# Block 3's y read back in two sets of partitions, the ranking's products behind the first second product, and the logits copied in two tiles

## The chip, the cores and the metric

The kernel runs on one core of one Trainium2 chip. The metric is the device time of one execution in microseconds (us); three runs were timed, and their median is the time before. TensorE (PE) does the matrix products, VectorE (DVE) and ScalarE (ACT) the elementwise work, GpSimd (POOL) the indirect transfers, and SyncE (SP) issues nearly all other DMAs. Each engine works through its own instructions in order.

## The reference, cut to what matters

```
h   = x + conv(layernorm(x)) + D_skip * layernorm(x)      # x: 2048 tokens x 512, S4D kernel applied by FFT
xt  = layernorm(h)
g   = softmax(xt @ wg)                                    # 8 experts
e   = argmax(g)                                           # one expert for each token
out = h + (gate / gate) * gelu(xt @ w1[e]) @ w2[e]        # w1: 512 x 1792, w2: 1792 x 512 for each expert
```

## The kernel before, in words

Two layers follow each other in one program. The convolution works on four blocks of 128 channels. For a block, four steps `c_s1` (matmul line L502) and eight steps `c_s2` (L521) transform the S4D kernel, `c_z` (DVE, L712) multiplies with the transformed input that `c_load` (SP, L705) read into a tile `u`, `c_ia` (PE, L719 and L720) transforms back, `c_ys` copies the result out of PSUM (ACT or DVE, L725), and `c_yst` (SP, L728) stores it in the DRAM scratch `yd`. The eight pieces of a block are called rc 0 to 7, and the store of rc fills 16 consecutive rows of the layout in which y is read back. In block 3 the pieces are made in the order 5, 7, 2, 6, 3, 0, 1, 4.

When all eight stores of the block have landed, `c_y1` (SP, L751) reads y back in four quarters q of 512 KB, each a tile of 128 partitions. `c_ib` (PE, L756, four matmuls) does the last transform of a quarter, `c_add` (DVE, L759) adds it to the residual, and the routing work follows: `r_s4` and `r_ag` (DVE, L972 and L1018) gather statistics, `r_tr` (PE, L977) transposes, `r_ev` (ACT, L981) copies, `r_lg` (PE, L989) makes logits, and `r_hd` (SP, L1003) stores h in the scratch `hd`. Block 3's quarters go in the order 0, 2, 1, 3. Quarters of block 2 stand beside them.

Behind the last logits `r_le` (L995) copies them out of PSUM in two halves, one on ACT and one on DVE, into two halves of one tile; `r_lt` (PE, L1000) transposes them, `r_sd` (ACT, L1022) takes square roots of the variances, `r_rs` (DVE, L1025) inverts them, and `r_vs` (SP, L1077) stores mean and inverse deviation in `hd`. A chain on DVE and PE (L1053 to L1161) picks each token's expert and makes the row list `r_gi` of the first expert. `m_ga` (POOL, L1266) gathers the rows of that expert from `hd`, so it waits for the list and for all stores into `hd`.

Then come eight experts. `m_w1` and `m_w2` (SP, L1349 and L1359) load weights, `m_h` (ACT, L1363) and `m_l` (DVE, L1367) split them in two parts, `m_ln`, `m_tr`, `m_xh` and `m_xl` (L1311, L1317, L1324, L1329) prepare the tokens, `m_g1` (PE, L1376 to L1378) makes first products, `m_ge`, `m_gh` and `m_gl` (L1381, L1384, L1388) the gelu and its split, and `m_g2` (PE, L1409 to L1411) second products. Beside the first expert the rest of the ranking is done: `r_B` and `r_M` (DVE, L1148 and L1169), `r_tb` (PE, L1176, 16 matmuls in two calls) and `r_ix` (DVE, L1180 to L1184), which gives the row lists of the other experts.

The order of the work is written out by hand. `ORD` gives every call of a step a number; all calls are emitted by rising number, and so each engine and each queue gets its order. `ON` chooses ACT (A) or DVE (V) for a copy. `FILL` puts filler matmuls (`idle`, PE, L930) ahead of a step: the number is a count of 128-column matmuls on zeros or the identity. The lists that `plan.add` takes as `r` and `w` name what a step reads and writes; the waits themselves follow from tiles and DRAM regions. A tile with a `tag` shares its `bufs` buffers with all tiles of that tag: the weights' tiles `h2` and `l2` give room to y of block 3, and `l2` to the logits.

Of the kernel before, what the change touches and what calls it, by code (L numbers as in the profile page):

```python
# [85 lines left out]
def _dram(ap, dims, off=0):  # L86
# [3 lines left out]
ORD = {  # L90
    'm_hold2': [932.5],
# [59 lines left out]
    'c_load': [422, 414, 333, 383, 331, 379, 398, 328, 530, 557, 455, 495, 452, 518, 439, 510, 591, 674, 686, 648, 657, 588, 645, 602,  # L151
# [4 lines left out]
    'c_s2': [437, 429, 373, 401, 370, 397, 413, 365, 555, 577, 486, 516, 489, 536, 481, 532, 635, 688, 710, 661, 678, 630, 656, 628, 805,  # L156
        809, 783, 795, 815, 774, 790, 779],
    'c_z': [444, 438, 386, 407, 375, 403, 428, 368, 563, 584, 496, 521, 491, 569, 485, 542, 641, 694, 714, 667, 691, 634, 664, 631, 810,
        812, 789, 799, 820, 777, 794, 785],
    'c_ia': [451, 446, 391, 417, 378, 408, 433, 374, 571, 593, 509, 526, 506, 579, 490, 552, 644, 703, 721, 680, 700, 639, 670, 652, 819,  # L160
        822, 798, 800, 825, 786, 811, 793],
    'c_ys': [456, 453, 399, 424, 384, 425, 441, 380, 582, 604, 517, 531, 512, 606, 499, 558, 654, 716, 730, 687, 709, 646, 675, 662, 823,
        826, 807, 813, 829, 788, 817, 796],
    'c_yst': [460, 458, 402, 426, 387, 430, 445, 381, 585, 607, 519, 533, 515, 610, 504, 561, 659, 717, 734, 690, 712, 651, 677, 663,
        824, 827, 808, 816, 830, 792, 818, 797],
# [17 lines left out]
    'r_ag': [863, 870.7, 870.6, 870.8],  # L183
# [3 lines left out]
    'm_w1': [818.5, 871, 871.5, 944, 951, 974, 979, 1009, 1032, 1050, 1088, 1099, 1120, 1146, 1166, 1186, 1202, 1222, 1247, 1269, 1291, 1313, 1331, 1347, 1367, 1393, 1416, 1436, 1452, 1474, 1490, 1522, 1539, 1559, 1580, 1596, 1617, 1633, 1662, 1678, 1698, 1723, 1736, 1757, 1773, 1801, 1817, 1840, 1852, 1873, 1889, 1905, 1932, 1948, 1968, 1978],  # L187
# [40 lines left out]
    'r_tb': [962.5, 974.5],  # L228
# [85 lines left out]
def s4d(tc, plan, env, cst, x, log_ar, a_im, c_re, c_im, log_dt, d_skip):  # L314
# [376 lines left out]
    cv = {}  # L691
# [69 lines left out]
    def conv(blk):  # L761
# [124 lines left out]
def moe(tc, plan, env, cst, wg, w1, w2, out):  # L886
# [578 lines left out]
    def tasks():  # L1465
# [4 lines left out]
        for b4 in range(4):  # L1470
# [3 lines left out]
            at("A", 0.2, r_sd, b4, w=[f"val/0/{b4}"], tab="sqrt")  # L1474
# [181 lines left out]
```

## Time and profile before

| what | us |
|---|---|
| median of the three timed runs | 726.71 |
| lowest and highest of them | 723.38 and 727.33 |
| the profiled execution's own time | 719.45 |
| span from its first to its last instruction | 717.4 |
| busy: PE, PE weight loads, DVE, ACT, POOL | 656.3, 575.3, 562.7, 455.7, 81.5 |

All rows below come from that one profiled execution. Times in them are microseconds from the start of the span. A PE row's length reaches over the start of the next row because matmuls are pipelined, so the spacing of starts tells what a group costs. "SPq" and "DMA_DIRECT2D" rows are the issuing of a transfer, not the transfer. A wait for several events is put down to the one that came last, as far as the trace can tell. A granted clock of 1.00 is TensorE's upper level (2.4 GHz), 0.50 the lower one (1.2 GHz).

### The profile page before, as it was taken

How to read it: one execution, taken by the hardware profiler on the slowest of the kernel's cores; microseconds unless marked ns; L12 is line 12 of the kernel's file. 1: busy time of each engine (PE TensorE's matmuls, PEld its weight loads, DVE VectorE, ACT ScalarE, POOL GpSimd, SP SyncE). 2: the span in 40 equal slices, each digit the busy share in tenths (PEclk: the TensorE clock that was granted, in tenths of full speed). 3: DMA queues.
4: the chain of work that ended last, by engine and by line, in shares of the span. 5: the costliest groups of instructions: out<-in, count | busy, mean ns of one | idle time of the engine just before them, and what ended most of it. 6: DMA issues, size and time to landing. Idle time of an engine off the chain costs nothing.

```text
span 717.4 us, 19936 instructions
## 1 busy us (share of the span) xinstructions
PE 656.3 (91%) x8192; PEld 575.3 (80%) x8192; DVE 562.7 (78%) x1055; ACT 455.7 (64%) x909; POOL 81.5 (11%) x65
## 2 busy tenths in 40 slices
PE   3588999988989999798889999999999999999995
PEld 2346898768778877596479999999999989898884
DVE  6999998889999999666689866766766687666752
ACT  6899999968974977312445555464555456566651
POOL 0000000000000000000006041050320402133201
PEclk9699999999999999999999999999999999999998
DMA  9994134566666678898767565465564667576620
GB/s 188 171 228 78 63 119 179 190 256 200 183 170 199 224 226 256 245 290 258 193 231 226 165 209 177 150 213 174 174 210 150 205 209 258 179 238 200 204 89 27
DMA packets 139255, 136.38 MB, mean 190 GB/s; under 512 B 42171, under 2 KB 108351, under 8 KB 138906
## 3 DMA queue, kind: packets, MB, share of 16 engines
q1 hardware_dynamic: 135674, 126.48, 60.7%
q0 software_dynamic: 3488, 8.60, 3.6%
q8 instruction: 65, 1.06, 0.6%
q14 instruction: 28, 0.23, 0.1%
HBM read 109.83 MB, written 29.52 MB: 194 GB/s over the span
## 4 chain that ended last, share of the span: by engine, by line
PE 43%; issue 17%; DVE 15%; DMA 12%; ACT 5%; SPq 4%; POOL 2%; POOLq 1%; DVEq 0%; ACTq 0%
DMA y<-yd_scratch 5%; PE ps_s L1376 4%; PE ps_s L1378 4%; PE ps_s L1377 4%; PE ps_kk L521 3%; DMA yd_scratch<-ys 3%; PE pk L652 2%; PE ps_ga L719 2%; DMA hr<-hd_scratch 2%; PE ps_ga L720 2%; PE ps_pl L930 2%; PE ps_kk L1409 2%; PE ps_s L502 2%; SPq L366 2%; PE ps_kk L1411 2%
## 5 line engine op out<-in xcount | busy, mean ns | idle before, releaser
L1367 DVE TENSOR_TENSOR l<-r,h 128x1024 fp32r<-128x1024 f32 x112 | 135.8, 1220 | 45.1 <-ACT h L1363 44.7
L1363 ACT CAST h<-r 128x1024 fp32r<-128x1024 f32 x112 | 116.1, 1047 | 45.7 <-PE ps_ga L1411 22.6
L1376 PE MATMUL ps_s<-xh,h 128*128 128x288 f32 (+5 forms) x448 | 128.7, 287 | 0.0
L1378 PE MATMUL ps_s<-xl,h 128*128 128x288 f32 (+5 forms) x448 | 127.3, 284 | 0.0
L1377 PE MATMUL ps_s<-xh,l 128*128 128x288 f32 (+5 forms) x448 | 127.1, 284 | 0.0
L1381 ACT ACTIVATE g<-ps_s 128x288 f32<-128x288 f32 (+5 forms) x112 | 43.6, 389 | 93.4 <-PE ps_s L1378 77.1
L1376 PEld LDWEIGHTS ps_s<-xh,h 128*128 128x128 f32 x448 | 84.5, 189 | 2.8 <-ACT xh L1324 0.2
L1377 PEld LDWEIGHTS ps_s<-xh,l 128*128 128x128 f32 x448 | 84.5, 189 | 2.2 <-issue 0.2
L1378 PEld LDWEIGHTS ps_s<-xl,h 128*128 128x128 f32 x448 | 84.4, 188 | 0.0
L1388 DVE TENSOR_TENSOR gl<-g,gh 128x288 fp32r<-128x288 f32 (+5 forms) x112 | 46.6, 426 | 23.0 <-ACT gh L1384 21.5
L719 PE MATMUL ps_ga<-u,mi 128*128 128x128 f32 x256 | 51.0, 281 | 3.1 <-issue 2.4
L1259 POOL DMA_INDIRECT out_dram<-ot,si x20 | 29.1, 1455 | 213.9 <-DVE ot L1426 210.4
L589 ACT ACTIVATE e<-alp 128x128 f32<-128x128 f32 x256 | 53.3, 313 | 0.0
L930 PE MATMUL ps_pl<-ident 128*128 128x512 f32 (+1 forms) x156 | 52.6, 483 | 0.0
L720 PE MATMUL ps_ga<-u,mi 128*128 128x128 f32 x256 | 49.8, 275 | 0.5 <-issue 0.5
L719 PEld LDWEIGHTS ps_ga<-u,mi 128*128 128x128 f32 x256 | 38.8, 191 | 7.7 <-issue 4.6
L930 PEld LDWEIGHTS ps_pl<-ident 128*128 128x128 f32 x156 | 27.5, 211 | 20.5 <-issue 19.7
L712 DVE TENSOR_TENSOR u<-ps_kk,u 128x1024 f32<-128x1024 f32 x32 | 38.5, 1216 | 4.9 <-PE ps_kk L521 4.8
L720 PEld LDWEIGHTS ps_ga<-u,mi 128*128 128x128 f32 x256 | 38.9, 192 | 0.6 <-issue 0.6
L1384 ACT CAST gh<-g 128x240 fp32r<-128x240 f32 (+5 forms) x82 | 33.6, 410 | 8.2 <-PE ps_ga L1410 5.4
L652 PE MATMUL pk<-e,vr 128*32 128x64 f32 x1024 | 36.1, 230 | 2.8 <-issue 1.6
L652 PE MATMUL pk<-wi,vi 128*32 128x64 f32 x1024 | 36.3, 228 | 2.2 <-DVE vi L628 1.1
(289 smaller groups left out, 1587.4 us busy)
## 6 DMA issues: line engine op xcount, KB each, us to landing
r<-in_B_w_dram SPq DMA_DIRECT2D x112, 512.0 KB, 3.8
u<-ud_scratch SPq DMA_DIRECT2D x32, 512.0 KB, 5.5
ud_scratch<-xn SPq DMA_DIRECT2D x16, 512.0 KB, 3.9
yd_scratch<-ys SPq DMA_DIRECT2D x32, 256.0 KB, 5.5
y<-yd_scratch SPq DMA_DIRECT2D x16, 512.0 KB, 5.0
xu<-in_A_u_dram SPq DMA_DIRECT2D x16, 256.0 KB, 7.2
xd_scratch<-in_A_u_dram SPq DMA_DIRECT2D x8, 512.0 KB, 7.2
xr<-xd_scratch SPq DMA_DIRECT2D x6, 512.0 KB, 4.1
```

The source lines that it names most:

```text
L589: A.activation(tb[blk, "e"][:, l // 2, :, l % 2], par(alp, blk), AF.Exp, scale=float(l))
L652: T.matmul(pk[32 * g:32 * g + 32, 64 * j:64 * j + 64], v[:, :, 8 * g + j], w[:, :, 8 * g + j, :], start=n == 0, stop=n == 1, skip_group_ch ...
L719: T.matmul(pa[:, c], mi[:, 4 * rc + rr, 64:192], z[:, 0, c], start=True, stop=False)
L720: T.matmul(pa[:, c], mi[:, 4 * rc + rr, 0:128], z[:, 1, c], start=False, stop=True)
L930: T.matmul(p[:, 0:128 * k], w, _view(ident, [[0, k], [1, 128]]), start=first, stop=True, skip_group_check=True)
L1363: A.copy(tile_(("h" + n, e, f), list(r.shape), F32R, pool="wp", name="h" + n, bufs=3 if n == "1" else 2), r)
L1367: V.tensor_tensor(tile_(("l" + n, e, f), list(r.shape), F32R, pool="wp", name="l" + n, bufs=3 if n == "1" else 2), r, t_["h" + n, e, f].bi ...
L1376: T.matmul(o[:, 0:CAPS[e]], a, xh, start=c == 0, stop=False)
L1377: T.matmul(o[:, 0:CAPS[e]], b, xh, start=False, stop=False)
L1378: T.matmul(o[:, 0:CAPS[e]], a, xl, start=False, stop=c == 3)
L1381: A.activation(tile_(("g", e, f), [128, CAP], name="g", bufs=2)[:, 0:CAPS[e]], t_["pf", e, f][:, 0:CAPS[e]], AF.Gelu_apprx_tanh)
L1388: V.tensor_tensor(tile_(("gl", e, f), [128, CAP], F32R, name="gl", bufs=3)[:, 0:n], t_["g", e, f][:, 0:n], t_["gh", e, f][:, 0:n].bitcast( ...
```

## The change

1. In block 3 the pieces rc 2 and rc 4 change places: the order becomes 5, 7, 4, 6, 3, 0, 1, 2, so that the last three pieces fill rows 0 to 47 of y. Their loads and u tiles change places too. The copy `c_ys` of rc 4, now third, goes to DVE; that of rc 2, now last, was on DVE already.
2. Each quarter of block 3's y is read in two transfers. `c_ya` reads partitions 48 to 127 (320 KB), which rc 3 to 7 fill; for q 0, 2 and 1 ACT issues it (ahead of `m_h(0)`), for q 3 SP does, behind the last store. `c_y1` then reads partitions 0 to 47 (192 KB) on SP, where the whole reads stood.
3. `r_tr`, `r_ev` and `r_lg` of block 2's quarter 1 move from behind block 2's last additions to 766.5, 766.6 and 773.5, around the last `c_s1` of block 3. Two fillers of 3 (ahead of `c_s1` 15 and of block 3's first `c_s2`) go.
4. `r_sd` is one activation on all 16 columns behind `r_le` instead of four, the first of which stood among the quarters of block 3; a new `r_sq` on one column stands at 830.6, behind `m_h(0)`.
5. `r_le` writes two tiles, and both copies are on ACT.
6. `m_w1(2)`, the load of expert 0's third piece of w1, moves on SP's queue from ahead of `r_vs` to behind it (871.5 to 905.3).
7. `r_tb` moves from ahead of the first `m_g2` to behind it (962.5 to 969.5), its second call from ahead of the fifth `m_g1` to behind it (974.5 to 975.5).
8. In block 3, `r_lg` of q 0 goes behind the last `c_ib` (865 to 868.2), `r_s4` of q 1 behind the last `c_add` (866.5 to 869.5), the first `r_ag` from 863 to 864.5.

```
 ORD = {
+    'r_sq': [830.6],
+    'r_sd': [883.5],
+    'c_ya': [829.1, 829.3, 829.2, 830.3],
...
-    'r_sd': [863.4, 883.4, 883.3, 883.5],
...
 FILL = {
...
-    ('c_s1', 10): 5, ('c_s1', 11): 5, ('c_s2', 23): 4, ('c_ib', 9): 9, ('c_s1', 15): 3, ('c_s2', 29): 3, ('c_ib', 12): 4, ('r_p1', 0): 8,
+    ('c_s1', 10): 5, ('c_s1', 11): 5, ('c_s2', 23): 4, ('c_ib', 9): 9, ('c_ib', 12): 4, ('r_p1', 0): 8,
...
     def c_load(blk, rc):
-        u = cv["u1", blk, rc] = utile(blk == 3 and rc > 2)
+        u = cv["u1", blk, rc] = utile(blk == 3 and rc not in (0, 1, 4))
...
     def c_y1(blk, q):
 
         if blk < 3 and (blk, q) != (2, 3):
-            t = cv["y1", blk, q] = mp.tile([128, 2, 512], F32, name="y1")
-        else:
-            t = cv["y1", blk, q] = env["wp"].tile([128, 2, 512], F32, name="y3", tag=("h2", "l2")[q // 2], bufs=2)
-        nc.sync.dma_start(t, _dram(yd, [[32 * 128, 128], [16 * 128, 2], [1, 512]], (blk * 32 * 128 + 4 * q) * 128))
+            cv["y1", blk, q] = mp.tile([128, 2, 512], F32, name="y1")
+        elif blk < 3:
+            cv["y1", blk, q] = env["wp"].tile([128, 2, 512], F32, name="y3", tag=("h2", "l2")[q // 2], bufs=2)
+        y1(nc.sync, blk, q, 0, 48 if blk == 3 else 128)
+
+    def c_ya(q):
+        cv["y1", 3, q] = env["wp"].tile([128, 2, 512], F32, name="y3", tag=("h2", "l2")[q // 2], bufs=2)
+        y1(nc.sync if q == 3 else nc.scalar, 3, q, 48, 128)
+
+    def y1(eng, blk, q, a, b):
+        eng.dma_start(cv["y1", blk, q][a:b], _dram(yd, [[32 * 128, b - a], [16 * 128, 2], [1, 512]], (blk * 32 * 128 + 4 * q) * 128 + 32 * 128 * a))
...
     def r_le(ev, b4):
-        if "ls" not in t_:
-            sm("ls", [128, 512], pool="wp", tag="l2", bufs=2)
-        ev(t_["ls"][:, 256 * b4:256 * b4 + 256], t_["pl"][:, 256 * b4:256 * b4 + 256])
+        t_["ls"] = t_["ls", b4] = env["wp"].tile([128, 256], F32, name="r_ls", tag="l2", bufs=2)
+        ev(t_["ls", b4], t_["pl"][:, 256 * b4:256 * b4 + 256])
...
-    def r_sd(b4):
-        v = t_["val"][:, 4 * b4:4 * b4 + 4, 1]
+    def r_sq():
+        A.activation(sm("sq", [128, 1]), epsc, AF.Sqrt)
+
+    def r_sd():
+        v = t_["val"][:, :, 1]
         A.activation(v, v, AF.Sqrt, bias=epsc)
```

## Rows read from the trace of the kernel before

**Rows 1.** The part of the chain of waits between 285 and 345 us (start us, us, what).

```profile
303.72 16.44 DMA hr<-hd_scratch
...
322.52 0.49 PE ps_ga L719 x2
...
331.97 2.57 DMA yd_scratch<-ys
```

**Rows 2.** The timeline of TensorE (PE) between 331 and 350 us: start us, us, engine, line, operation, tiles, shape, count, and in brackets the idle time before it with what ended it.

```profile
331.25 1.94 PE L756 MATMUL ps_s<-y,ibc 128*64 128x512 f32 x8
...
337.49 1.12 PE L930 MATMUL ps_pl<-ident,zero 128*128 128x512 f32 x2
...
339.29 1.08 PE L756 MATMUL ps_s<-y,ibc 128*64 128x512 f32 x4 [0.67 <-DMA y<-yd_scratch]
...
341.21 1.08 PE L756 MATMUL ps_s<-y,ibc 128*64 128x512 f32 x4 [0.84 <-DMA y<-yd_scratch]
...
342.22 0.66 PE L977 MATMUL ps_ga<-ident,h 128*128 128x128 f32 x4
...
342.81 1.08 PE L756 MATMUL ps_s<-y,ibc 128*64 128x512 f32 x4
...
343.82 0.43 PE L989 MATMUL ps_pl<-ys,wgp 128*32 128x128 f32 x8
...
344.17 0.66 PE L977 MATMUL ps_ga<-ident,h 128*128 128x128 f32 x4
...
348.10 0.43 PE L989 MATMUL ps_pl<-ys,wgp 128*32 128x128 f32 x8 [0.37 <-ACT ys L981]
```

**Rows 3.** The timeline of ScalarE (ACT) between 325 and 357 us, columns as before.

```profile
332.23 1.04 ACT L1363 CAST h<-r 128x1024 fp32r<-128x1024 f32 x1 [0.28 <-DMA r<-in_B_w_dram]
...
333.81 1.08 ACT L981 COPY ys<-ps_ga 128x512 f32<-128x512 f32 x2 [0.54 <-PE ps_ga L977]
...
343.57 1.28 ACT L1022 ACT_TABLE_LOAD   x1
...
348.59 0.37 ACT L995 COPY r_ls<-ps_pl 128x256 f32<-128x256 f32 x1 [0.55 <-PE ps_pl L989]
...
355.68 0.31 ACT L1065 ACTIVATE r_lg<-r_lg 128x128 f32<-128x128 f32 x1
```

**Rows 4.** The timeline of SyncE's queue (SPq) between 310 and 365 us; its times are those of issuing.

```profile
315.29 5.12 SPq L728 DMA_DIRECT2D yd_scratch<-ys  x2
...
334.67 2.49 SPq L751 DMA_DIRECT2D y<-yd_scratch  x4
...
347.01 1.12 SPq L1349 DMA_DIRECT2D r<-in_B_w_dram  x2
...
349.86 0.57 SPq L1077 DMA_DIRECT2D hd_scratch<-r_val  x1
```

**Rows 5.** DMA seen in three ways: the landing of the one y store that SyncE issues at 325.2 us (view of its line in 325.0 to 325.8 us), the issues by line between 320 and 365 us (KB each, median us to landing), and two stretches in the table of windows (length, busy time and count of PE, PEld, DVE, ACT and POOL, granted TensorE clock, share of the 16 DMA engines, GB/s).

```profile
DMA to landing us min/median/max: 5.7/5.7/5.7
...
hd_scratch<-r_val SPq DMA_DIRECT2D x1, 32.0 KB, 5.8
...
330.00:332.00 2.00, 2.00 (x16) 1.47 (x17) 0.00 (x0) 0.59 (x1) 0.00 (x0) 1.00 1.04 337
...
332.00:334.00 2.00, 2.00 (x14) 1.00 (x10) 1.45 (x3) 1.23 (x2) 0.00 (x0) 1.00 0.71 219
...
334.00:336.00 2.00, 1.76 (x24) 0.99 (x23) 2.00 (x7) 1.34 (x3) 0.00 (x0) 1.00 0.04 5
```

**Rows 6.** The hand-off to the first gather: the timelines of VectorE (DVE) and GpSimd (POOL).

```profile
348.99 0.42 DVE L995 COPY r_ls<-ps_pl 128x256 f32<-128x256 f32 x1 [0.34 <-ACT r_ls L995]
...
349.95 0.29 DVE L1053 TENSOR_REDUCE r_mx<-ps_kk 128x16 f32<-128x128 f32 x1
...
355.33 0.16 DVE L1161 TENSOR_REDUCE r_gi<-ps_kg 128x3 int32<-128x6 f32 x1 [0.23 <-PE ps_kg L1157]
...
376.72 0.35 DVE L1184 TENSOR_REDUCE r_gi<-r_ge 128x24 int32<-128x192 f32 x1
...
356.70 0.97 POOL L1266 DMA_INDIRECT rows<-hd_scratch,r_gi  x1 [47.22 <-ACT r_lg L1065]
...
377.85 0.98 POOL L1266 DMA_INDIRECT rows<-hd_scratch,r_gi  x1 [17.74 <-DVE gl L1388]
```

**Rows 7.** The same table of windows for four other stretches.

```profile
302.44:305.85 3.41, 3.41 (x67) 3.07 (x70) 0.69 (x1) 0.59 (x1) 0.00 (x0) 0.50 1.01 225
...
370.40:372.10 1.70, 0.00 (x0) 0.00 (x0) 1.67 (x6) 0.39 (x1) 0.00 (x0) 1.00 0.87 298
...
372.10:402.00 29.90, 29.89 (x252) 29.79 (x252) 28.80 (x82) 16.04 (x27) 11.49 (x9) 1.00 0.63 196
...
402.00:404.00 2.00, 1.17 (x11) 1.00 (x10) 2.00 (x4) 0.27 (x1) 0.00 (x0) 1.00 0.07 26
```

**Rows 8.** Who waited for whom: DVE between 364 and 403 us, then PE between 363 and 404 us (us in total, times, longest us); below them one row of PE's timeline at 302 us.

```profile
DVE xl L1329 <- ACT xh L1324: 0.3, 1, 0.3
...
PE ps_pl L1176 <- DVE r_M L1169: 1.7, 1, 1.7
...
PE ps_kg L1317 <- DVE xl L1329: 0.8, 1, 0.8
...
302.40 1.22 PE L502 MATMUL ps_s<-s1c,kt 64*64 64x64 f32 x33 [2.16 <-issue]
```

More of the change, by code (lines that the diff above doesn't have):

```diff
@@ L155 @@
     'm_load': [337, 336, 340, 347, 346, 339, 345, 341],
[L156 to L165, printed above, removed]
+    'c_s2': [437, 429, 373, 401, 370, 397, 413, 365, 555, 577, 486, 516, 489, 536, 481, 532, 635, 688, 710, 661, 678, 630, 656, 628, 805, 809, 815, 795, 783, 774, 790, 779],
+    'c_z': [444, 438, 386, 407, 375, 403, 428, 368, 563, 584, 496, 521, 491, 569, 485, 542, 641, 694, 714, 667, 691, 634, 664, 631, 810, 812, 820, 799, 789, 777, 794, 785],
+    'c_ia': [451, 446, 391, 417, 378, 408, 433, 374, 571, 593, 509, 526, 506, 579, 490, 552, 644, 703, 721, 680, 700, 639, 670, 652, 819, 822, 825, 800, 798, 786, 811, 793],
+    'c_ys': [456, 453, 399, 424, 384, 425, 441, 380, 582, 604, 517, 531, 512, 606, 499, 558, 654, 716, 730, 687, 709, 646, 675, 662, 823, 826, 829, 813, 807, 788, 817, 796],
+    'c_yst': [460, 458, 402, 426, 387, 430, 445, 381, 585, 607, 519, 533, 515, 610, 504, 561, 659, 717, 734, 690, 712, 651, 677, 663, 824, 827, 830, 816, 808, 792, 818, 797],
     'c_y1': [507, 467, 487, 523, 653, 636, 619, 679, 780, 738, 756, 804.3, 838, 843, 841, 846],
@@ L169 @@
     'r_hd': [528, 500, 514, 559, 684, 660, 640, 708, 858.2, 757, 784, 858.4, 858.1, 867, 863, 870.5],
-    'r_tr': [529, 539, 541, 560, 685, 719, 729, 739, 833.5, 831.2, 831.4, 834.5, 859, 876, 866.2, 879],
-    'r_ev': [534, 548, 545, 562, 689, 725, 736, 742, 833.7, 831.3, 831.6, 834.7, 862, 876.5, 867, 879.5],
-    'r_lg': [538, 551, 550, 600, 713, 731, 741, 745, 836, 833.3, 834.2, 837, 865, 880, 877, 882],
+    'r_tr': [529, 539, 541, 560, 685, 719, 729, 739, 833.5, 766.5, 831.4, 834.5, 859, 876, 866.2, 879],
+    'r_ev': [534, 548, 545, 562, 689, 725, 736, 742, 833.7, 766.6, 831.6, 834.7, 862, 876.5, 867, 879.5],
+    'r_lg': [538, 551, 550, 600, 713, 731, 741, 745, 836, 773.5, 834.2, 837, 868.2, 880, 877, 882],
     'open_l': [752],
-    'r_s4': [833, 755, 782, 840, 858, 866.5, 864, 870],
+    'r_s4': [833, 755, 782, 840, 858, 869.5, 864, 870],
     'r_ld': [761, 791, 804, 770],
@@ L264 @@
     'c_ev1': 'AVAAAAAAAVVVVAAVAAVVVVAAAAVVAVAV',
-    'c_ys': 'AVAAAAVAVAAAAVVAAAAAAAAAVVVAAAAA',
+    'c_ys': 'AVAAAAVAVAAAAVVAAAAAAAAAVVVAVAAA',
     'r_ev': 'AAAAAAVAAAAAAAAA',
     'r_cb': 'V',
-    'r_le': 'AV',
+    'r_le': 'AA',
     'r_c8': 'V',
@@ L774, in conv @@
             j = f"/{8 * blk + rc}"
-            u = ("u3" if last and rc > 2 else "u1") + j
+            u = ("u3" if last and rc not in (0, 1, 4) else "u1") + j
             at("S", 1.46, c_load, blk, rc, r=[f"ud{n}/{rc}", "main/0"] + ["h3/0/o"] * (u[1] == "3") + [f"ld/{blk - 1}"] * (blk > 0), w=[u, f"ld{n}/{rc}"])
@@ L787, in conv @@
             if last:
-                at("S", 1.46, c_y1, blk, q, r=["hw/0/o", f"yd{n}"], w=[ys[q], f"yl/0/{q}"])
+                at("S" if q == 3 else "A", 0.6, c_ya, q, r=["hw/0/o"] + [f"yd{n}/{rc}" for rc in range(3, 8)], w=[ys[q] + "/a"])
+                at("S", 1.46, c_y1, blk, q, r=[f"yd{n}"], w=[ys[q] + "/b"])
             else:
@@ L999, in r_lt @@
             t_["lt"] = bank("kk")
-        T.transpose(t_["lt"][:, 128 * b4:128 * b4 + 128], t_["ls"][:, 128 * b4:128 * b4 + 128], ident)
+        T.transpose(t_["lt"][:, 128 * b4:128 * b4 + 128], t_["ls", b4 // 2][:, 128 * (b4 % 2):128 * (b4 % 2) + 128], ident)
     def r_hd(blk, b4):
@@ L1473, in tasks @@
             at("V", 0.43, r_ag, b4, r=[f"st_/{b4}"], w=[f"val/0/{b4}"])
-            at("A", 0.2, r_sd, b4, w=[f"val/0/{b4}"], tab="sqrt")
+        at("A", 0.2, r_sq, r=["hw/0/o"], tab="sqrt")
+        at("A", 0.2, r_sd, w=["val/0"], tab="sqrt")
         at("V", 0.15, r_tk, r=["rc_/0", "hw/0/o"], w=["val/0/t"])
@@ L1479, in tasks @@
         for h in range(2):
-            at("AV", (0.4, 0.4), r_le, h, r=[f"plt/0/{2 * h}", f"plt/0/{2 * h + 1}", "hw/0/o"], w=[f"ls/0/{h}"])
+            at("AV", (0.4, 0.4), r_le, h, r=[f"plt/0/{2 * h}", f"plt/0/{2 * h + 1}", "hw/0/o"], w=[f"ls/{h}"])
         for b4 in range(4):
-            at("T", 0.25, r_lt, b4, r=[f"ls/0/{b4 // 2}"], w=[f"ltx/0/{b4}"])
+            at("T", 0.25, r_lt, b4, r=[f"ls/{b4 // 2}"], w=[f"ltx/0/{b4}"])
         at("V", 1.5, r_a, r=["ltx/0", "rc_/0"], w=["oh/0", "mx/0"])
```

8 lines of the change are left out of this document (4 added, 4 removed), and 1 row of the table ORD.

## The prediction

> **What bounds the kernel now.** I read the chain of waits first, then the timelines of the stretch that the diff touches, then the windows behind it.
>
> Around block 3 the chain runs over DMA and PE. A statistics load lands at 303.72 + 16.44 = 320.16, DVE works through what queued behind it, and PE goes on at 322.52 [rows 1]. The last piece's store is issued at 331.97 and lands 2.57 later, at 334.54 [rows 1]; SP then issues four reads of y in 2.49 us from 334.67 [rows 4]. PE waits for the first until 339.29 and for the second again 0.84, until 341.21; from there it has work until the last logit product at 348.10 [rows 2], which runs until 348.46 (0.36, as derived below). Next come a copy, a DVE chain from 349.95 to the row list at 355.49, and the first gather at 356.70 [rows 6]. Nothing hides these steps: each waits for the one before.
>
> Behind the gather DVE bounds the kernel up to 403: between 364 and 403 it waited once, for 0.3 [rows 8], and it is busy 28.80 of 29.90 us [rows 7]. PE waits 1.7 for DVE's `r_M` and 0.8 for DVE's `xl` at about 403 [rows 8]. Later PE is the bound, so what the gather gains reaches the end one for one, and what PE alone gains before 403 does not.
>
> **Part by part.** *Order of pieces, copies, fillers, moved transposes (parts 1 and 3).* Loads and stores keep their sizes. A copy costs 0.55 to 0.6 on ACT [rows 3], and DVE's is taken as the same. PE loses six filler matmuls and gets four transposes and a logit product, 0.6 + 0.36, around 303 to 307. I cost all this at 0: PE meets the landing of 320.16 at 322.52 in either case [rows 1]. Without that cover it would be worth some 0.5 either way (two fillers of three 128-column matmuls against 0.96).
>
> *The split reads (part 2).* ACT's three issues wait for the store issued at 325.2; it landed 5.7 later, at 330.9 [rows 5]. No issue by ACT stands in the trace. SP's cost 0.62 (2.49 / 4) with an empty queue and 2.56 (5.12 / 2) in a full one [rows 4]; nothing can make one free. I take 0.6, since the DMA share falls from 1.04 at 330 to 332, to 0.71, to 0.04 at 334 to 336 [rows 5], and ACT's own queue is empty. SP's read of q 3 waits for block 2's `c_ib`, done by 333.2 (331.25 + 1.94) [rows 2]; behind it wait only the second reads, which need 334.54 anyway.
>
> Behind ACT's issues wait `m_h(0)`, `r_sq` and block 2's copies, for these PE's logits and filler, and then `c_ib`. Step by step: issues until 330.9 + 3 x 0.6 = 332.7; `m_h(0)` 1.04 until 333.75; table load 1.28 and square root 0.30 until 335.3; the first copy 0.55 until 335.9 [rows 3]. PE then does a logit product (0.36) and a transpose (0.59) until 336.85, ACT the copy until 337.5, PE the product until 337.9 and the filler (1.1) until 338.95. Before, the filler was through at 338.6 (337.49 + 1.12) [rows 2]: PE is ready 0.35 later, which matters only if y is there by then.
>
> When is it? The second read of q 0 is issued 0.13 behind the last store's landing, as now. Its 192 KB can't be quicker than the 256 KB store, 2.57 [rows 1], nor by its size slower than the whole read, 4.62 (334.67 to 339.29) [rows 2, 4]. I take 3.3, a little below the middle, since a read looks slower than a store and 3/8 remain. So q 0 is there at 334.54 + 0.13 + 3.3 + c = 337.97 + c; the next follow 0.62 apart, faster than PE consumes them (1.01).
>
> c is what the early reads cost the last store. At least 0: nothing brings it forward. At most the three reads' own time, 0.98 MB at the 337 GB/s of the full stretch [rows 5], 2.9. I take 0.9: all but the last store are issued before the reads, and the engines stood idle for most of 334 to 336. q 0 then comes at 338.9, level with PE.
>
> A rule speaks for more. By the Trainium skill (DMA: Bandwidth & Descriptors, Issuing engines are not separate DMA queues) transfers issued by different engines run on the same 16 DMA engines and interleave. Sharing evenly, two stores of some 0.8 us each (256 KB at 337 GB/s) that were still to move would take twice as long, c about 1.6, and the forecast would lose 0.6. No row here shows two such queues at once.
>
> From the start S of q 0's `c_ib` PE has four `c_ib` at 1.01, four transposes at 0.59 and four logit products at 0.36 (spacings of the rows at 342.22 to 344.17), 7.8 together, and 0.37 of wait ahead of the last product [rows 2]; with rounding 8.3. Before it was 339.29 + 0.84 + 8.3 = 348.46. With S = 338.95 it is 347.25: **1.2 gained**. Bounds: S = 338.95 at best, since PE isn't ready earlier; 340.8 at worst (c = 2.9), a loss of 0.7.
>
> *Part 8* reorders inside this sum: nothing.
>
> *Logits in two tiles, square roots together (parts 4 and 5).* Now DVE's copy starts 0.40 after ACT's (348.59, 348.99) because it waits for it [rows 3, 6]; ACT starts its next instruction 0.27 after the copy. The chain starts 0.15 earlier; bounds 0 and 0.2. The table load of 1.28 at 343.57 [rows 3] stood beside PE work and its removal frees nothing on the path.
>
> *The weight load behind `r_vs` (part 6).* `r_vs` is issued at 349.86 and lands 5.8 later, at 355.7 [rows 4, 5], behind two loads of 512 KB. The row list is ready at 355.49. Another gather starts 0.78 after its list (377.07 to 377.85) [rows 6]; from 355.49 that makes 356.27, against 356.70: **0.43** is `r_vs`. With one load fewer ahead (at 337 GB/s 1.6) it lands before the list. Bounds 0 and 0.43. The moved load delays a split on ACT that DVE uses only after the gather.
>
> *The ranking behind the second product (part 7).* PE's stall of 1.74 is filled with 1.5 us of products. I cost it at 0: DVE is full until 403, and PE will wait for `xl` longer there, 0.83 + 1.5.
>
> **Sum:** 1.2 + 0.15 + 0.43 = 1.8. The profiled execution's 719.45 becomes 717.65 (span 717.4 to 715.6). It stands 7.3 below the median of the timed runs, to which I apply the difference: 726.71 - 1.8 = **724.9**.
>
> **Rivals.** *A. The early reads hold up the last store fully*, c = 2.9: -0.7 + 0.58 = 0.1 slower, 726.8. For it: the full DMA until 332. Against: the idle stretch behind. 0.17.
>
> *B. ACT's issues are long, slower.* If an issue costs 2.56 as SP's did in the full queue, ACT is 3 x 1.96 = 5.9 later, and with it PE: S = 344.8, the sum 1.8 - 5.9 = 4.1 slower, 730.8. It decides from S = 340.7 on, where the whole gain of 1.8 is eaten, that is from 1.2 for an issue. Against: ACT's queue holds nothing else. 0.10.
>
> *C. The gather waits for ACT.* The trace puts its wait down to ACT's exponential [rows 6], which ends at 355.99 [rows 3]. After the change the load behind `r_vs` ends those three transfers, at 355.7 - 1.2 = 354.5; split 1.04, table 1.28 and exponential 0.31 give 357.1 and a gather at 357.8, 1.1 later than now: 727.8. Against: `r_vs` explains the start as well, and nothing of the exponential is gathered. 0.10.
>
> *D. The clock.* PE stood 2.16 idle, and the next 3.41 us ran at a granted 0.50 [rows 7, 8]; 1.74 idle at 370 left it at 1.00 [rows 7]. If the stall at 403 grows to 2.3 in one piece, 3.41 us at the lower level cost 1.7: 726.6. Against: part of it will fall on earlier waits. 0.10.
>
> *E. PE keeps what part 7 gives*, another 1.5: 723.4. For it: the stall is real. Against: DVE's full rows. 0.10.
>
> *F. The change does nothing*, because PE's readiness, not y, sets S: if the step-by-step sum for ACT is 1.2 short, only parts 5 and 6 remain, 726.1. 0.08.
>
> **Chances.** The forecast has 0.35, its own range 724.4 to 725.8 (c up to 1.9, and half a microsecond of scatter); A to F hold 0.65. Half a per cent is 3.6 us, about what a measurement of this kernel can tell from no change. Most cases lie inside it. Faster by more, below 723.1: E with some luck, and single runs that lie 4 us apart, 0.17. Slower by more, above 730.3: B, 0.11. Within: 0.72. The range, 721.5 to 729, holds all but B's end and that scatter.
>
> **What would show it.** Right: the first `c_ib` of block 3 starts at about 339 without a wait of PE between the quarters; the last logit product at about 347; the gather 0.8 behind its list; PE's wait for `r_M` gone and that for `xl` near 403 longer by as much. Wrong: a last store that lands 2 us or more after 334.5, issues by ACT above 1.2, a gather far behind its list, a stretch at 0.50 around 400, or PE without a longer wait at 403.

## The result and the profile after

| | before | after |
|---|---|---|
| median (lowest to highest), 20 runs each, taken together | 724.21 us (718.31 to 727.33) | 727.30 us (724.25 to 731.64) |
| ratio, with its 95% interval | 1 | 1.0053 (1.0035 to 1.0070) |
| own time of the profiled execution | 719.45 us | 728.13 us |
| span | 717.4 us | 726.4 us |

The kernel became slower, by 0.53% of 724.21, which is 3.8 us (the ratio is the one on record; the two medians themselves lie 3.1 apart). The forecast was 1.8 us faster. One run of e1 below (730.03 us) is left out as slow, over 1.5% above the fastest of its kernel.

The spans of the two profiled executions lie 9.0 us apart, and not all of that is the change. The last store of block 3 is issued at 335.63 instead of 331.97 [rows 1], 3.66 later, and 4.05 are there already at a product of block 2 (300.33 for 296.28), ahead of the reads and of the moved products. The kernel of experiment e10 is the changed one in everything it does up to that store, and there the store is issued at 331.14. So these 3.7 us belong to single executions, and from here on I count from the last store's issue. From it to the end of the span it is 717.4 - 331.97 = 385.4 us before and 726.4 - 335.63 = 390.8 after: 5.3 more.

SyncE's queue after the change (start us, us of issuing, what): the last store, and the four second reads, which wait until it has landed.

```profile
335.63 0.36 SPq L724 DMA_DIRECT2D yd_scratch<-ys  x1
...
340.73 2.51 SPq L754 DMA_DIRECT2D y<-yd_scratch  x4
```

Between the store's issue and the first read behind it lie 5.10 us. Before it was 2.70 (331.97 to 334.67) [rows 1, 4]. So the store landed 2.4 later: c, the price of the early reads for the store.

ScalarE in the same stretch:

```profile
334.97 1.98 ACTq L754 DMA_DIRECT2D y<-yd_scratch  x3
336.99 1.05 ACT L1369 CAST h<-r 128x1024 fp32r<-128x1024 f32 x1 [7.88 <-DMA yd_scratch<-ys]
338.06 1.28 ACT L1024 ACT_TABLE_LOAD   x1
339.35 0.20 ACT L1024 ACTIVATE r_sq<-repsc 128x1 f32<-128x1 f32 x1
339.46 1.05 ACT L985 COPY ys<-ps_ga 128x512 f32<-128x512 f32 x2
```

Three issues cost 0.66 each. Behind them come the cast and the square root's table load, which stood at 343.57 before [rows 3], and only then the two router copies that TensorE needs. TensorE:

```profile
336.67 1.09 PE L981 MATMUL ps_ga<-ident,xr 128*128 128x128 f32 x8
340.08 0.53 PE L993 MATMUL ps_pl<-ys,wgp 128*32 128x128 f32 x8 [2.32 <-ACT ys L985]
...
342.97 2.08 PE L934 MATMUL ps_pl<-ident,zero 128*128 128x512 f32 x2
346.59 3.68 PE L759 MATMUL ps_s<-y,ibc 128*64 128x512 f32 x8 [1.54 <-DMA y<-yd_scratch]
...
350.92 1.08 PE L759 MATMUL ps_s<-y,ibc 128*64 128x512 f32 x4
...
356.21 0.43 PE L993 MATMUL ps_pl<-ys,wgp 128*32 128x128 f32 x8 [0.38 <-ACT ys L985]
```

Three things are to be seen here. TensorE stands still for 2.32 us in front of ACT's copies. The first product with the fixed matrix starts 5.86 us after its second read was issued (346.59 - 340.73); for the whole read it was 4.62 [rows 2, 4]. And the filler takes 2.08 where it took 1.12 [rows 2], and two products 3.68 where two took 1.94 at 331.25 [rows 2]: half speed. The windows say so (length; busy time and count of PE, PEld, DVE, ACT and POOL; granted clock; share of the DMA engines; GB/s):

```profile
340.27:350.51 10.24, 8.55 (x40) 2.68 (x33) 1.75 (x6) 0.83 (x2) 0.00 (x0) 0.50 0.81 156
...
341.00:348.00 7.00, 5.31 (x26) 1.50 (x26) 0.00 (x0) 0.58 (x1) 0.00 (x0) 0.50 1.01 183
...
411.95:415.36 3.41, 3.41 (x18) 3.41 (x17) 2.19 (x4) 0.80 (x2) 0.00 (x0) 0.50 0.55 168
```

From 340.27 on, 0.2 us after that wait ended, TensorE was granted its lower level (0.50, 1.2 GHz) for 10.24 us, and again for 3.41 us at 412, 1.5 us after a wait for `xl` had ended:

```profile
410.45 0.41 PE L1323 MATMUL ps_kg<-ident,hn 32*128 32x32 f32 x4 [1.85 <-DVE xl L1335]
```

The middle row of the windows is the other half of the story: while y is read, the DMA engines are fully occupied (1.01) and move 183 GB/s. While the whole reads ran, they moved twice that, in the kernel before:

```profile
339.00:344.00 5.00, 3.87 (x24) 1.17 (x24) 3.22 (x14) 1.01 (x2) 0.00 (x0) 1.00 1.04 366
```

The first product thus comes 10.96 us after the last store's issue in place of 7.32, and the last router product 20.58 (356.21 - 335.63) in place of 16.13: 4.45 of the 5.3 are lost in this stretch. The first product alone is 3.64 late: 2.40 by the store and 1.24 by the read (5.86 for 4.62). The other 0.81 arise between it and the third product (350.92 - 346.59 = 4.33, where it was 342.81 - 339.29 = 3.52 [rows 2]), while TensorE ran at half speed. From the third product to the last router product both kernels take 5.29. The hand-off to the gather is as forecast; VectorE and GpSimd:

```profile
357.88 0.29 DVE L1059 TENSOR_REDUCE r_mx<-ps_kk 128x16 f32<-128x128 f32 x1
...
363.26 0.16 DVE L1167 TENSOR_REDUCE r_gi<-ps_kg 128x3 int32<-128x6 f32 x1 [0.22 <-PE ps_kg L1163]
...
364.31 0.97 POOL L1272 DMA_INDIRECT rows<-hd_scratch,r_gi  x1 [52.01 <-DVE r_gi L1167]
```

The gather starts 0.89 after the row list (363.42), where it took 1.21 [rows 6], and it waits for the list now.

### The profile page after: what moved, and what is told of

Read it like the earlier page. It is cut to its first block, busy times and chain, and to the rows that moved or that the text cites. A ratio compares the mean times of both kernels' runs of the same rounds, so it can differ in the third digit from the quotient of the medians.

```text
span 726.4 us, 19919 instructions
## 1 busy us (share of the span) xinstructions
PE 661.0 (91%) x8180; PEld 576.5 (79%) x8180; DVE 563.1 (78%) x1055; ACT 455.0 (63%) x907; POOL 82.0 (11%) x65
## 4 chain that ended last, share of the span: by engine, by line
PE 26%; issue 14%; DVE 6%; POOL 2%; POOLq 1%; DMA 1%; ACT 0%; DVEq 0%
PE ps_s L1383 4%; PE ps_s L1382 4%; PE ps_s L1384 4%; DVE l L1373 2%; PE ps_kk L1415 2%; PE ps_ga L1415 2%; PE ps_kk L1416 2%; PE ps_kk L1417 2%; PE ps_ga L1417 2%; PE ps_ga L1416 2%; POOLq L1452 1%; POOL out_dram L1265 1%; DVE gl L1394 1%; POOL cwt L1272 1%; DMA rows<-hd_scratch,r_gi 1%
## 5 line engine op out<-in xcount | busy, mean ns | idle before, releaser
L934 PE MATMUL ps_pl<-ident 128*128 128x512 f32 (+1 forms) x156 | 54.5, 496 | 0.0
L648 PEld LDWEIGHTS pk<-e,vr 128*32 128x32 f32 x1024 | 33.5, 144 | 7.0 <-issue 5.1
```

Source lines behind the costliest of these rows:

```text
L648: T.matmul(pk[32 * g:32 * g + 32, 64 * j:64 * j + 64], v[:, :, 8 * g + j], w[:, :, 8 * g + j, :], start=n == 0, stop=n == 1, skip_group_ch ...
L934: T.matmul(p[:, 0:128 * k], w, _view(ident, [[0, k], [1, 128]]), start=first, stop=True, skip_group_check=True)
```

## The experiments

The eleven kernels were timed in five rounds each beside the kernel before, in four sittings, and each ratio is to that sitting's own runs of before. This table gathers them. "To c_ib", "to router" and "to end" are counted from the start of the last store's issue (its row in SyncE's queue) to the start of the first product with the fixed matrix in block 3, to the start of the last router product, and to the end of the span, in the one profiled execution of each kernel. "Half clock" is the time at a granted 0.50 between that store and 353 us, in us, from windows of 1 us and to the nearest half.

| kernel | median us (runs) | before in the same sitting | ratio (95%) | to c_ib | to router | to end | half clock |
|---|---|---|---|---|---|---|---|
| before | | | 1 | 7.32 | 16.13 | 385.4 | 0 |
| after | 727.30 (20) | 724.21 | 1.0053 (1.0035, 1.0070) | 10.96 | 20.58 | 390.8 | 10 |
| e1 | 722.00 (11) | 721.25 | 1.0020 (0.9994, 1.0045) | 6.89 | 16.53 | 384.3 | 0 |
| e2 | 726.57 (6) | 721.25 | 1.0076 (1.0052, 1.0100) | 10.33 | 19.87 | 389.7 | 3.5 |
| e3 | 725.18 (12) | 721.25 | 1.0060 (1.0037, 1.0084) | 11.09 | 21.04 | 390.2 | 10 |
| e4 | 721.13 (12) | 721.25 | 1.0003 (0.9979, 1.0027) | 7.53 | 16.60 | 384.7 | 0 |
| e5 | 726.51 (7) | 721.33 | 1.0065 (1.0041, 1.0089) | 11.06 | 20.45 | 391.2 | 3.5 |
| e6 | 723.41 (12) | 721.33 | 1.0038 (1.0014, 1.0062) | 9.68 | 19.51 | 388.7 | 3.5 |
| e7 | 730.55 (6) | 721.33 | 1.0128 (1.0097, 1.0159) | 11.00 | 20.70 | 388.8 | 7 |
| e8 | 723.19 (12) | 721.33 | 1.0025 (1.0003, 1.0048) | 8.79 | 18.25 | 389.2 | 7 |
| e9 | 721.09 (12) | 722.00 | 0.9984 (0.9958, 1.0010) | 7.23 | 15.94 | 386.2 | 0 |
| e10 | 723.05 (12) | 722.00 | 1.0037 (1.0005, 1.0068) | 9.85 | 18.67 | 386.9 | 0 |
| e11 | 719.09 (12) | 721.06 | 0.9972 (0.9945, 0.9999) | 6.70 | 14.94 | 384.9 | 0 |

**Which part loses: e1 to e4.** Four kernels take the change apart. e1 is the changed kernel with part 2 undone:

```
-    'c_ya': [829.1, 829.3, 829.2, 830.3],
...
-        y1(nc.sync, blk, q, 0, 48 if blk == 3 else 128)
+        y1(nc.sync, blk, q, 0, 128)
```

> The changed kernel with part 2 undone: each quarter of block 3's y is one read again, issued by SyncE behind the last store; every other part stays. Theory 1 (the split reads are the cost: they hold up the last store and move slowly themselves): the last store lands about 2.6 us after its issue instead of 5.0, block 3's first c_ib starts 4.6 us after the first read's issue as in the kernel before, and the time is 4 to 5 us below the changed kernel's, level with the kernel before or up to 1 us below it. Theory 2 (the ranking's move costs, by the lower clock near 412 us): the time stays at least 1 us above the kernel before. Theory 3 (the shift of 4 us that the two traces show already at 300 us belongs to the change): the time stays 3 us or more above the kernel before.

e2 is the kernel before with parts 1 and 2 alone (the diff of e1 the other way round, and the order of the pieces).

> The kernel before with parts 1 and 2 alone (order of block 3's pieces, y read in two sets of partitions). Theory 1: 3 to 5 us above the kernel before; the last store lands 4.5 to 5 us after its issue, the four early reads land some 2 us apart, and TensorE's clock falls to 0.50 while it waits. Theory 2 and theory 3 (the reads are harmless): within 1 us of the kernel before.

e3 is the changed kernel with part 7 undone:

```
-    'r_tb': [969.5, 975.5],
+    'r_tb': [962.5, 974.5],
```

> The changed kernel with part 7 undone: r_tb ahead of the first second product again. Theory 1: TensorE's stall of 1.7 us ahead of r_tb is back, the wait for xl near 403 is about 0.8 us again, no stretch at 0.50 there, and the time is 0 to 1.5 us below the changed kernel's, still 2 to 4 us above the kernel before. Theory 2 (the ranking's move is most of the loss): 3 us or more below the changed kernel, level with the kernel before. Should the move gain time after all, this is 1 us or more above the changed kernel.

e4 is the kernel before with parts 4, 5, 6 and 8.

> The kernel before with parts 4, 5, 6 and 8 alone (square roots together, logits in two tiles on ScalarE, one weight load behind r_vs, three steps reordered). By the prediction's own terms 0.6 us below the kernel before (0.15 of the copies, 0.43 of r_vs), with the first gather 0.8 to 0.9 us after its row list instead of 1.2. Rival (the square root's table load of 1.3 us now stands ahead of block 2's copies and delays TensorE): level with the kernel before or up to 1 us above it.

The split reads alone cost 0.76%, and with them undone the rest of the change can't be told from before. e4 can't either, and e3 is like the changed kernel. So the loss comes from part 2, as closely as the intervals can tell (e1's reaches up to 1.0045). The 0.6 us that the prediction's terms gave e4 don't show in its time. Its one trace has 0.7 us less from the store to the end (384.7 against 385.4), although its router product comes 0.47 later than before: as the rival said, TensorE waits for ACT's copies behind the table load, 1.19 us where it was 0.24:

```profile
336.73 0.43 PE L997 MATMUL ps_pl<-ys,wgp 128*32 128x128 f32 x8 [1.19 <-ACT ys L989]
```

e2's rows, ScalarE, SyncE's queue and TensorE:

```profile
331.91 1.98 ACTq L753 DMA_DIRECT2D y<-yd_scratch  x3
```

```profile
332.17 0.36 SPq L723 DMA_DIRECT2D yd_scratch<-ys  x1
...
337.29 2.52 SPq L753 DMA_DIRECT2D y<-yd_scratch  x4
```

```profile
342.50 3.30 PE L758 MATMUL ps_s<-y,ibc 128*64 128x512 f32 x8 [2.82 <-DMA y<-yd_scratch]
```

The same picture as after, without the other parts: 5.12 us until the store has landed and the second reads go out, 5.21 more until the first product, and half speed in the products behind it.

**Why the reads are slow: e5 and e6.** The kernel before, with each whole read of block 3's y made in two reads of half its bytes, behind the last store. All first halves go before all second ones, eight reads in the same order in both kernels. They differ in one line:

```
     def y2(q, s):
         o = (3 * 32 * 128 + 4 * q) * 128
-        nc.sync.dma_start(cv["y1", 3, q][64 * s:64 * s + 64], _dram(yd, [[32 * 128, 64], [16 * 128, 2], [1, 512]], o + 32 * 128 * 64 * s))
+        nc.sync.dma_start(cv["y1", 3, q][s:128:2], _dram(yd, [[2 * 32 * 128, 64], [16 * 128, 2], [1, 512]], o + 32 * 128 * s))
```

The first line is e5 (a block of 64 neighbouring partitions), the second e6 (every other partition).

> The kernel before with one thing altered: each of block 3's four whole reads of y (128 partitions, landing about 1.5 us apart: 339.25, 341.17, 342.42, 343.71 in the trace of before) is made as two reads of half its bytes, all on SP and behind the last store, first partitions 0 to 63 of all four tiles, then partitions 64 to 127 of all four. Theory P (a read over a block of neighbouring partitions gets only part of the way into SBUF, so that half the bytes take as long as the whole did): the eight reads land about 1.5 us apart each, the last near 339 + 7 x 1.5 = 350, some 6 us later than before; time 4 to 6.5 us over before. Theory N (what costs is that there are eight reads instead of four, 0.62 us of issue each): the last read lands about 8 x 0.62 + 3.3 = 8.3 us after the first issue, near 343 to 344, and the time is 0.5 to 2.5 us over before, like e6_every_other. The Trainium skill, 'SBUF - State Buffer', section 'Door 1: The DMA port swizzle', says that a transfer's bandwidth depends on how many of 16 ports its partitions reach, and its table gives partitions 0 to 63 eight of them; it speaks for P.

> As e5_halves, with the same count of reads, the same bytes in each and the same order of issue, but the first four reads take the even partitions of each tile and the last four the odd ones. Theory P: reads spread over all partitions land 0.6 to 0.8 us apart, the last one near 344, and the time is 0 to 2 us over before, at least 3 us under e5_halves. Theory N: the same as e5_halves within 1 us, in the landings and in the time.

Windows of e5, then of e6, while the reads run (columns as above):

```profile
342.00:350.00 8.00, 3.60 (x10) 0.65 (x8) 1.17 (x4) 0.00 (x0) 0.00 (x0) 0.81 0.93 187
```

```profile
339.50:344.50 5.00, 1.97 (x6) 0.31 (x6) 0.00 (x0) 0.00 (x0) 0.00 (x0) 1.00 0.95 313
```

187 GB/s against 313, with the same count of reads and the same bytes in each: half a read into 64 neighbouring partitions takes as long as the whole read did. The times follow: by the medians e5 is 5.2 us over before, e6 2.1. Their intervals overlap, so between these two it is the windows that decide. The Trainium skill, "SBUF — State Buffer", section "Door 1: The DMA port swizzle", has this: bandwidth goes by how many of 16 ports the partitions reach, partitions 0 to 63 reach only eight, and a transfer into them was measured there at 196 GB/s. The trace of e5 agrees, with 187. One rival is left between e5 and e6: the line alters the rows of DRAM that a read takes too, neighbouring ones in e5 and every other one in e6. e8 below settles it, since its reads take 64 neighbouring rows, as those of e5 do, into every other partition. What e6 still loses lies at the start of the stretch: its first tile is complete only with the fifth read, its first product comes 9.68 us after the last store's issue, and 3.5 us at half speed follow.

**Is it the store that was held up: e7.** The changed kernel, with the early reads all on SP and behind the last store:

```
-    'c_ya': [829.1, 829.3, 829.2, 830.3],
+    'c_ya': [830.1, 830.3, 830.2, 830.4],
...
-        y1(nc.sync if q == 3 else nc.scalar, 3, q, 48, 128)
+        y1(nc.sync, 3, q, 48, 128)
```

> The changed kernel with the four early reads of partitions 48 to 127 all issued by SP right behind the last store, none by ACT, so that nothing of them is ahead of the store. Theory A (the loss is the last store's landing, 5.02 us from its issue in place of 2.57, because the early reads run beside it): the store lands 2.4 to 2.9 us after its issue, the second reads are issued 2 us sooner, and the time falls by 2 to 3 us to about the forecast, 1.000 to 1.002 of before. Theory P (the reads of 80 and of 48 partitions are each about as slow as a whole one): the store lands early, but the eight reads follow one another at 1 to 2 us each as before, the first tile is complete no earlier than 5.5 us after the second read's issue, and the time stays within 1.5 us of the changed kernel, 1.003 to 1.007 of before.

SyncE's queue, TensorE, and a window while the reads run:

```profile
336.00 0.36 SPq L724 DMA_DIRECT2D yd_scratch<-ys  x1
...
339.31 2.47 SPq L754 DMA_DIRECT2D y<-yd_scratch  x4
```

```profile
347.00 1.08 PE L759 MATMUL ps_s<-y,ibc 128*64 128x512 f32 x4 [2.40 <-DMA y<-yd_scratch]
```

```profile
340.00:348.00 8.00, 5.21 (x34) 1.64 (x34) 0.54 (x3) 1.21 (x3) 0.00 (x0) 0.79 1.04 209
```

The second reads go out 3.31 us after the store's issue, 1.8 sooner than in the changed kernel, and yet the first product comes 11.00 us after it, as in the changed kernel (10.96): what the store gained, the second read lost, 7.69 us from issue to product. So letting the store through gains nothing; the slow transfers cost the same, whoever waits for them. This trace also shows the two kinds of read one after the other, mainly those of partitions 48 to 127 and then those of 0 to 47:

```profile
341.20:345.50 4.30, 3.20 (x19) 0.80 (x18) 0.00 (x0) 0.59 (x1) 0.00 (x0) 0.60 1.07 229
...
345.50:348.50 3.00, 1.17 (x6) 0.32 (x8) 0.37 (x1) 0.00 (x0) 0.00 (x0) 0.93 1.01 142
```

At 229 GB/s 320 KB take 1.4 us, at 142 GB/s 192 KB take 1.4, and at 366 GB/s the whole 512 KB took 1.4 (estimates from the windows). The time rose further, to 1.0128, which no theory foresaw. The one trace is of the lowest of its six runs (726.68 to 732.18), so what the other five did is not seen; this stays open.

**With all partitions reached: e8.** As e7, but the early reads fill the odd partitions and the second reads the even ones; the fixed matrix's rows are permuted alike.

```
+        nc.sync.dma_start(cv["y1", 3, q][s:128:2], _dram(yd, [[32 * 128, 64], [16 * 128, 2], [1, 512]], (3 * 32 * 128 + 4 * q) * 128 + 32 * 128 * 64 * s))
...
-            T.matmul(po[64 * h:64 * h + 64, :], ibc, cv["y1", blk, q][:, h, :], start=True, stop=True)
+            T.matmul(po[64 * h:64 * h + 64, :], amp[:, 0:64] if blk == 3 else ibc, cv["y1", blk, q][:, h, :], start=True, stop=True)
```

> As e7_behind_store, but the early reads bring rows 64 to 127 of y (pieces 4 to 7) into the odd partitions and the second reads rows 0 to 63 (pieces 0 to 3, the last four made) into the even ones, with the 64 columns of the fixed matrix permuted alike for block 3 (loaded once more, 32 kB, with block 3's x). Count and order of the reads are those of e7, 64 and 64 partitions in place of 80 and 48. Theory P: the early reads land 0.6 to 0.9 us apart and the first tile is complete 3 to 3.8 us after its second read's issue (5.86 in the changed kernel, 4.62 for the whole read of before): the time is 3 to 5 us under e7 and 1 to 1.5 us under e1_whole_reads, 0.997 to 1.000 of before. Theory N (eight reads cost more than four, wherever their partitions lie): within 1 us of e7.

A window while the early reads run, and TensorE's first products:

```profile
336.00:340.00 4.00, 3.40 (x26) 1.19 (x22) 0.74 (x4) 0.62 (x2) 0.00 (x0) 0.71 0.95 316
```

```profile
341.00 3.65 PE L767 MATMUL ps_s<-y,amp 128*64 128x512 f32 x8 [1.22 <-issue]
```

316 GB/s in place of 209: the reads are fast again. The time is 7.4 us below e7's, more than the reads account for, since to the router product the two traces differ by 2.45 us; the rest belongs to what stayed open in e7. And it is no gain over before, where 0.997 to 1.000 was expected. The first product comes after 8.79 us, 5.69 from the issue of the second reads (335.31) and not 3 to 3.8; that the four early reads stand ahead of them is the likely reason, but no run tests it. The two products then run at half speed.

**What the clock takes: e10.** The changed kernel with fillers where TensorE stood still:

```
-    ('c_s1', 10): 5, ('c_s1', 11): 5, ('c_s2', 23): 4, ('c_ib', 9): 9, ('c_ib', 12): 4, ('r_p1', 0): 8,
+    ('c_s1', 10): 5, ('c_s1', 11): 5, ('c_s2', 23): 4, ('c_ib', 9): 9, ('r_lg', 10): 8, ('c_ib', 12): 12, ('r_p1', 0): 8,
```

> The changed kernel with more idle products on TensorE: 8 units ahead of the router product that waited 2.32 us for ACT's copies at 340.08, and 12 in place of 4 ahead of block 3's first product with the fixed matrix, so that TensorE does not stand still in this stretch. Theory K (of the loss, 1.7 us is the half clock, under which the first two products took 3.68 us in place of the 1.94 that two took at 334.80): the granted clock stays at 1.00 from 336 to 352, the two products take about 2.0 us, and the time falls by 1.3 to 2 us, to 1.0025 to 1.0040 of before. Theory D (the reads set the pace; the products at half speed only fill the time until the next read has landed): the clock stays up, but the third product starts no sooner than 0.5 us before that of the changed kernel, against the last store's issue, and the time stays within 0.7 us, 1.0045 to 1.0065.

TensorE's first three products with the fixed matrix, and a window while the reads run:

```profile
340.99 1.08 PE L759 MATMUL ps_s<-y,ibc 128*64 128x512 f32 x4 [0.71 <-DMA y<-yd_scratch]
342.92 1.08 PE L759 MATMUL ps_s<-y,ibc 128*64 128x512 f32 x4 [0.85 <-DMA y<-yd_scratch]
...
344.51 1.08 PE L759 MATMUL ps_s<-y,ibc 128*64 128x512 f32 x4
```

```profile
336.00:342.00 6.00, 4.92 (x30) 1.68 (x28) 0.00 (x0) 0.59 (x1) 0.00 (x0) 1.00 0.86 191
```

The clock stays at 1.00 while the data move as slowly as in the changed kernel (191 GB/s). The third product starts 13.37 us after the last store's issue (344.51 - 331.14), against 15.29 in the changed kernel (350.92 - 335.63), 1.92 less. Not all of that is the clock. The first product comes 1.11 sooner after the store (9.85 for 10.96), and there TensorE stood waiting for the read in both traces (0.71 and 1.54 us), so its clock doesn't account for it; why this read came sooner is open. The other 0.81 lie between the first and the third product: 3.52, as in the kernel before, for 4.33. Without any wait for a read these products would take 2.61 at full clock (two of 1.01 and transposes of 0.59, spacings of [rows 2]), so of the changed kernel's 4.33 the half clock took between 0.8 and 1.7, an estimate. The last router product is still 2.5 behind that of before, and all of it is there at the first product (9.85 for 7.32). The time, 1.0037, lies where the first theory put it, but the interval reaches over both theories and over the changed kernel's 1.0053.

**A version of the reads that loses nothing: e9 and e11.** e9 is the kernel before with part 1's order of the pieces and e8's reads, but early ones only for tiles 0 and 2, whose products come first; behind the store follow the second halves of these two and then 1 and 3.

```
+    'c_ya': [830.1, 830.2],
...
+    def c_ya(i):
+        q = 2 * i
+        cv["y1", 3, q] = env["wp"].tile([128, 2, 512], F32, name="y3", tag=("h2", "l2")[q // 2], bufs=2)
+        y2(q, 1)
...
+            for k in range(1 + q % 2):
+                y2(q, k)
```

> Built on the kernel before: its parts 1 and 2 only, in another form. Every read of block 3's y takes every other partition (64 of 128) as in e8_spread; only tiles 0 and 2, whose two products come first, have an early read, issued by SP right behind the last store; when the store has landed follow the second reads of 0 and 2, then both halves of 1 and of 3. Theory L (what counts is when tiles 0 and 2 are complete, for TensorE is busy without a gap from the second product on: from 341.21 to 347.73 in before): with some 2.9 us from a read's issue to its first packet and 0.7 to 0.8 us for each half read, tile 0 is complete 6.3 to 7 us after the last store's issue (7.32 in before) and tile 2 some 0.7 us later (9.2 in before), so that the second product starts 1 to 1.9 us earlier against the last store: 0.9975 to 0.9990 of before. Theory B (what counts is the sum of bytes and the DMA engines' state after the stores; eight reads lose whatever their order): 1.001 to 1.005 as e6_every_other and e8_spread. If TensorE's granted clock falls to 0.5 in this stretch, as it did in e8_spread, the two first products take 3.6 us in place of 2.0 and the gain is gone whichever theory holds.

e11 adds parts 4, 5, 6 and 8, with the table load moved out of the way:

```
+    'r_sq': [815.5],
```

> The reads of e9_interleaved together with parts 4, 5, 6 and 8 of the change, with the square root of the small tile that loads the table (r_sq, 1.28 us of table load on ACT) put among ACT's idle time ahead of block 3's last pieces, where it is ahead of no router copy; parts 3 and 7 left out. Theory S (the two gains add up: the reads bring the last router product 0.2 us nearer to the last store, 15.94 us in place of 16.13, and the parts behind it take 0.7 to 1.2 us off the rest, from the last store's issue to the end, as e4_small_parts, 384.70 us, and e1_whole_reads, 384.25 us, against 385.43 us of before): 0.9970 to 0.9990 of before, 384 to 385 us from the last store's issue to the end. Theory N (both were inside the spread of single profiles): 0.9985 to 1.0015 and 385.4 us or more.

TensorE, ScalarE and GpSimd in e11:

```profile
334.86 0.43 PE L1001 MATMUL ps_pl<-ys,wgp 128*32 128x128 f32 x8 [0.24 <-ACT ys L993]
...
339.19 1.08 PE L766 MATMUL ps_s<-y,amp 128*64 128x512 f32 x4 [0.16 <-issue]
340.54 1.08 PE L766 MATMUL ps_s<-y,amp 128*64 128x512 f32 x4 [0.27 <-DMA y<-yd_scratch]
...
347.43 0.43 PE L1001 MATMUL ps_pl<-ys,wgp 128*32 128x128 f32 x8 [0.37 <-ACT ys L993]
```

```profile
322.75 1.28 ACT L1032 ACT_TABLE_LOAD   x1
```

```profile
355.42 0.97 POOL L1280 DMA_INDIRECT rows<-hd_scratch,r_gi  x1 [45.26 <-DMA r<-in_B_w_dram]
```

e9 can't be told from before. In e11 the second product starts 8.05 us after the last store's issue (9.24 before), the last router product 14.94 (16.13 before): 1.2 us gained in this trace, as much as the forecast had hoped of the split. In e9, with the same reads, it was 0.2, so one cannot say how much of it the reads bring and how much the other parts or the single execution. At 719.09 us (0.9972, 0.9945 to 0.9999) the time is 2.0 us below that of the kernel before, with an interval that just excludes no change. From the store to the end its trace shows 0.5 us less, within what the first theory said; behind the gather it has a stretch at the lower clock (0.57 on average between 371 and 375 us, where before has 1.00).

## Why the prediction was wrong

- **The step that failed is the second read's 3.3 us, and with it the bound under it:** "nor by its size slower than the whole read, 4.62". It is 5.86. The bound took a transfer's time to go by its bytes; e5 against e6 and e7 against e8 show that it goes by the partitions that the bytes fall into, 187 against 313 and 209 against 316 GB/s. In e7's windows 192 KB into partitions 0 to 47 and 320 KB into 48 to 127 each take about what 512 KB into all 128 do. The early reads, then, were not done when the second ones were issued: from 341 on the engines are full at 183 GB/s, and part of the 5.86 is time behind them; how much, no row tells. The prediction weighed how two queues share the engines, and not this.
- **c was mis-sized**, 2.4 in place of 0.9 (1.6 with even sharing), near rival A's 2.9. Of itself it would have cost 1.5. But e7 shows that it isn't a cost of its own: with the store let through, its time comes back in the reads. Rival A named the store's delay rightly and bounded it by 0.98 MB at 337 GB/s, the same wrong rate. With 5.86 for 3.3 and 2.4 for 0.9 the forecast's own sum for y, 337.97 + c, gives 342.93, which is the 10.96 us measured from the store to the first product.
- **The clock, rival D, was looked for at one place only**, the stall near 403. There the changed kernel did what it says: TensorE waited 1.85 us for `xl`, and 3.41 us at 0.50 followed at 411.95. Behind the last router product e1, e7, e8 and e10 have the same work as the changed kernel, and each has the same wait of 1.85; but only e8 has such a stretch behind it. From the last router product to the end (the table's "to end" less "to router") it takes 370.2 us in the changed kernel and 370.9 in e8, and 367.7 to 368.2 in the other three. So in these single traces the stretch goes with 2 to 3 us, more than rival D's 1.7, and outweighs what parts 4 to 8 gain over the 369.3 of before. How often it came in the timed runs is not known. The other place is 340, behind a wait of 2.32 us for ACT's copies, where the half clock took 0.8 to 1.7 (e10). The prediction had the steps on ACT, down to the table load ahead of the copies, and had TensorE ready 0.35 later than before. It looked only at whether y would be there first, not at what the idle time does to the clock.
- **Together**: from the store to the last router product the forecast was 16.13 - 1.2 = 14.9, and it is 20.6. Of the 4.45 over before, 3.64 are there at the first product, the held store and the slow read, and 0.81 come by the half clock behind it. The median of 727.30 lies inside the range 721.5 to 729, which is luck: the kernel before, in 20 runs, takes 724.21 and not the 726.71 that the forecast started from, and the change has the other sign.
- **Right** were the issue by ACT (0.66 each for 0.6 forecast; rival B falls), part 5 (`r_mx` starts 1.67 behind the last router product in place of 1.85: 0.18 for 0.15), part 6 in its mechanism (in e4 the gather follows the list by 0.77, for 0.78 forecast, where it was 1.21; rival C falls, since in the changed kernel the gather waits for the list and for nothing of ACT's), and part 7, costed at nothing: TensorE's wait for `r_M` shrank from 1.7 to 0.3 and that for `xl` grew from 0.8 to 1.9, and e3 shows no difference in time beyond its interval. Rival E falls with that, and F too: it was y that set the start, by 1.54 us of wait.

## What to carry to other kernels

When a transfer is split to start part of it early, see which partitions each part falls into: here a part that went into a block of neighbouring partitions took as long as the whole, so that the split doubled the time instead of hiding half of it, while parts that took every other partition kept most of the rate. Ask of every step that lets TensorE stand still for a microsecond or two, even with slack behind it, what the granted clock does next. And put a table load where its engine is idle anyway, not merely off the path by its own sum: TensorE waited 1.19 us for the copies behind it in e4, and 0.24 in e11, where the load had moved.

## What was not expected of the hardware

- The DMA engines' share says nothing of the rate: 1.01 at 183 GB/s in the changed kernel, 1.04 at 366 in the one before.
- From the last store's issue to the second reads that wait for it went 5.1 us in the changed kernel and in e2, where ACT had issued one read of 320 KB ahead of it and went on beside it, 6.2 in e10 (331.14 to 337.38), where it had issued two, and 3.3 in e7, where all reads stood behind the store; before it was 2.7.
- The clock fell after waits of 2.32 us (after), 4.40 (e5) and 3.03 (e6), and in e8 where 1.26 was the longest wait ahead of it; in e1, with waits of 1.18 and 1.67, it did not. Behind the same wait of 1.85 near 403 it fell in two of five traces of the same work. These rows give no bound by which one could have foreseen it.
